# Rebuilding the order of the first tile in a fused attention and feed-forward kernel

## The chip, the cores and the metric

The kernel runs on one core of one Trainium2 chip, as one launch. The metric is the device time of that launch in microseconds; lower is better. Five runs of the kernel before stand beside one profiled execution.

## The reference, cut to what matters

Block-causal attention over 8 batches of 8 heads, 576 positions and 64 elements a head (blocks of 64 positions), then a gated feed-forward layer on the same 4608 tokens. All inputs and the output are float32.

```python
scores = scale * np.matmul(q, k.transpose(0, 1, 3, 2))      # scale = 1/8
mask = (pos[:, None] // 64) >= (pos[None, :] // 64)
attn = softmax(np.where(mask, scores, -1e9))
x = np.matmul(attn, v).transpose(0, 2, 1, 3).reshape(4608, 512)
gate = np.maximum(x @ w_gate, 0.0)                          # w_gate, w_val: 512 x 1536
out = (gate * (x @ w_val)) @ w_out                          # w_out: 1536 x 512
```

## The kernel before

**Attention.** A *round* `r` is a pair of heads of one batch: batch `r // 4`, pair `hp = r % 4`. For 512 of the 576 positions it needs q and k with the head's elements on the partitions (`qTm`, `kTm`), computes scores transposed, takes exp on ACT into `attnT`, sets the corners that the mask forbids to zero (`corners`), multiplies with v (`head_av`, one head each; a column of ones beside v gives the sum), normalises on DVE (`normalise`: a reciprocal and a multiply into `xnat`), and transposes the result into `xT`, the input of the feed-forward layer. The last 64 positions of all batches are *tails*: `tail_visit`, `tail_av`, `xTt`.

**Feed-forward.** `ffn_gen` is a Python generator over nine tiles `j`: one for each batch's 512 positions and one for all tails. Each `next` puts one 128x512 matmul into PE's program, so a tile has 144 steps: for `f` in 0 to 11 four products for gate and four for val (one for each chunk `c` of `xT`, that is for each round of the batch), then four out-projections of twelve. ACT takes the relu of gate, DVE multiplies it with val into `hT`, DVE copies the out-projection to `ob`, which a DMA stores. Attention work of batch `j + 1` and later stands between these steps at positions that are written out by hand: `ffn(n)` goes on by `n` steps, and `run(base, events)` sorts pairs of position and function.

**The order is by hand on every engine**: `tc.manual_schedule` keeps the order in which the program emits instructions on PE, DVE, ACT, POOL and SP. An engine that waits holds all that is behind it. Semaphores between engines are set by the framework, which also orders two engines' accesses to one PSUM bank.

**PSUM** has eight banks: `sc` two tiles of two banks, `one` one bank, and `ffnp` three banks, which gate, val, out-projection, transposes, `head_av` and a part of each score visit share.

**Loads.** All early loads are issued on SP's queue in the order of need (batch 0, weights, batch 1, w_out, batch 2), land as float32 in ten `stage` buffers, and are cast to bf16 by an engine: `cast_qk`, `cast_v`, `cast_w`, mostly on POOL. A stage buffer is loaded again when its cast is done. From batch 3 or 4 on, loads are issued by POOL and cast by the DMA (`load_qkv`), and transposes are DMAs on SP (`dma_transposes`, `to_xT_dma`).

**Batch 0 and the first tile.** Rounds 0 to 3 are done before the feed-forward layer starts, in a loop over `r`: `scores_1`, `pe_mains` of the next round (transposes on PE, L281, copied by `evac` at L284), `scores_2`, `head_av` of an earlier round. `junk` puts matmuls on zeros into PE's program. The first step of tile 0 is position 0. Batch 1's `pe_mains` stand at positions 64, 68, 98 and 110, its `sort_v` (v loaded packed, put in order by matmuls with a selection matrix) at 72 and 116, rounds 4 to 7 at 76, 88, 100 and 118. The stores of tile 0 are issued by POOL, all others by ACT.

Lines that the following text names: L182 `cast_qk`, L195 `cast_v`, L281 and L284 `pe_mains`, L316 `load_qkv`, L363 `cast_w`, L426 scores of `visit`, L508 the multiply of `normalise`, L553 `head_av`, L573 to L578 `to_xT_pe`, L583 `to_xT_dma`, L615 gate and val products, L624 relu, L628 `hT`, L634 out-projection, L664 `junk`.

Of the kernel before, what the change touches and what calls it, by code (L numbers as in the profile page):

```python
# [17 lines left out]
def kernel(  # L18
# [10 lines left out]
    nc = tc.nc  # L29
# [36 lines left out]
    attnT = [consts.tile([128, 2, AW], BF, name=f"attnT{i}") for i in range(2)]  # L66
# [52 lines left out]
    class Early:  # L119
# [59 lines left out]
        def cast_qk(self, h0, n, engs):  # L179
            lo = 64 * (h0 % 4)  # L180
            for t in range(2):
                engs[t](  # L182
                    self.half(t, h0 // 4)[:, :, lo : lo + 64 * n].rearrange(
                        "p j (h d) -> p h j d", d=64
                    ),
                    self.st[t, h0].rearrange("p (h j d) -> p h j d", h=n, j=4),
                )
# [60 lines left out]
        def transpose(self, hg):  # L248

            for t in range(2):  # L250
                pm = sb.tile([128, 4, 2, 128], BF, name="perm", bufs=8)
# [23 lines left out]
        def pe_mains(self, hp, evac):  # L275
            for t in range(2):
# [3 lines left out]
                for j in range(4):  # L280
# [3 lines left out]
                evac[t](  # L284
                    (qTm, kTm)[t][self.b % 2][:, :, hp, :].rearrange(
                        "p c (n j) -> p c n j", j=4
                    ),
                    tp.rearrange("p (j c n) -> p c n j", j=4, c=4),
                )
# [96 lines left out]
    def scores_1(r):  # L386
        b, hp = divmod(r, 4)
        at = attnT[r % 2]
        sc = scores(b, hp, [(0, 0, True)])
        nc.scalar.activation(at[:, :, 0:512], sc, AF.Exp, scale=scale)  # L390
        sc = scores(b, hp, [(0, 1, True), (384, 3, True)])
        return lambda: nc.scalar.activation(
            at[:, :, 512:1024], sc, AF.Exp, scale=scale
        )

    def scores_2(r):
        at = attnT[r % 2]
        sc = scores(*divmod(r, 4), [(0, 2, True)])
        nc.scalar.activation(
            at[:, :, 1024:1280], sc[:, :, 0:256], AF.Exp, scale=scale  # L400
        )
# [10 lines left out]
    def visit(r):  # L412

        b, hp = divmod(r, 4)
        at = attnT[r % 2]
# [74 lines left out]
    def corners(r, eng):  # L490

        at = attnT[r % 2]
        for lo, n in ((0, 512), (896, 128)):
            two = at[64:128, :, lo : lo + 2 * n].rearrange("p g (c n) -> p g c n", c=2)
            eng.memset(two[:, :, :, 0:64], 0.0)

    def corner(r, c, eng):
        eng.memset(attnT[r % 2][64:128, :, BASE[c] : BASE[c] + 64], 0.0)
# [39 lines left out]
    def head_av(r, hh):  # L538
        b, hp = divmod(r, 4)
        h = 2 * hp + hh  # L540
        at = attnT[r % 2]
# [20 lines left out]

    def xT_of(b):
# [4 lines left out]
    def to_xT_pe(r, evac):  # L568
        b, hp = divmod(r, 4)
        br = psum_ffn.tile([128, 1024], BF, name="ffnp")  # L570
# [3 lines left out]
        if r == 3:  # L574
# [27 lines left out]
    def ffn_gen():  # L602
        for j in range(B + 1):
            hT = []
            x = xT_of(j) if j < B else xTt.rearrange("p b h n -> p h b n")
            for f in range(12):
                i, fo = f // 4, 128 * (f % 4)
                gate = psum_ffn.tile([128, 512], FP, name="ffnp")
                val = psum_ffn.tile([128, 512], FP, name="ffnp")
                steps = [(t, c) for t in range(2) for c in range(4)]  # L610
                if j == 0 and f == 0:

                    steps.sort(key=lambda tc_: tc_[1] == 3)
                for t, c in steps:
                    nc.tensor.matmul(  # L615
                        (gate, val)[t],
                        (wg, wv)[t][i][:, c, fo : fo + 128],
# [3 lines left out]
                    )  # L621
                    if (t, c) == (0, 3):
# [4 lines left out]
                h = sb.tile([128, 512], BF, name="hT", bufs=16)  # L627
# [40 lines left out]
    dve, act, pool = nc.vector.tensor_copy, nc.scalar.copy, nc.gpsimd.tensor_copy  # L668
    with tc.manual_schedule(engines={E.PE, E.DVE, E.Activation, E.Pool, E.SP}):
# [11 lines left out]
        e0.cast_qk(0, 2, (dve, act))  # L681
        e0.pe_mains(0, (dve, act))
        junk(2)
        constants(1, nc.gpsimd)
        for h0 in (2, 4, 6):
            e0.cast_qk(h0, 2, (pool, pool))
        for r in range(4):
            scores_1(r)()
            if r == 3:
                e0.cast_v(6, 2, pool)  # L690
# [246 lines left out]
```

## Time and profile before

| | us |
|---|---|
| median of five runs | 372.78 |
| lowest and highest | 372.62, 378.24 |
| the profiled execution, its own time | 372.62 |
| span of that execution in the trace | 370.8 |
| first feed-forward matmul (L615) | 20.36 |
| first step of tile 1 (L615) | 66.56 |
| busy in the span: PE, ACT, DVE, POOL | 357.5, 171.2, 170.1, 119.1 |

The page shows one execution on this core. A row of an engine in the 40 slices gives the busy share of each slice of 9.27 us in tenths. A row of a list of stretches begins with the stretch and its length, and has for PE, PEld, DVE, ACT and POOL busy time and count, then the granted clock, the DMA share and GB/s. A wait row names who waited for whom: total, times, longest. A timeline row has start, duration, engine, line, operation, tiles and shape, and in brackets the idle time before it and what ended that.

### The profile page before, as it was taken

To read this page: it belongs to the slowest core of one execution; us is meant where nothing else is said; L and a number is where in the kernel's file an instruction comes from. 1 tells how busy PE (TensorE), PEld (TensorE's weight loads), DVE (VectorE), ACT (ScalarE), POOL (GpSimd) and SP (SyncE) were. 2 spreads that over 40 slices of the span, in tenths; PEclk is the share of its full clock that TensorE was granted. 3 is DMA by queue.
4 is the path that set the end of the run, shared out by engine and by line. 5 is a ranking of instruction groups with operands and counts; after the bars stand their busy time and mean duration, and the time that the engine had idled before them with its cause. 6 is when DMAs were issued, how large, how long until landed. Compare 5 with 4: busy or idle time off the path is not lost.

```text
span 370.8 us, 7561 instructions
## 1 busy us (share of the span) xinstructions
PE 357.5 (96%) x3004; PEld 177.3 (48%) x3004; DVE 170.1 (46%) x392; ACT 171.2 (46%) x283; POOL 119.1 (32%) x156
## 2 busy tenths in 40 slices
PE   6799979999999999999999999999999999999995
PEld 2544445544555545444554455444544454444443
DVE  3634444447465544444445533555254443423422
ACT  5933745566536462466345544553465323302310
POOL 6688866356258084580076004000000000000000
PEclk9999999999999999999999999999999999999999
DMA  8999999969959899999799857545200220020013
GB/s 254 292 371 356 375 205 296 211 173 253 163 135 132 87 132 172 149 126 154 150 102 129 139 120 84 44 90 124 80 14 17 67 77 6 2 85 28 3 38 104
DMA packets 140739, 51.35 MB, mean 138 GB/s; under 512 B 120352, under 2 KB 133920, under 8 KB 140704
## 3 DMA queue, kind: packets, MB, share of 16 engines
q0 software_dynamic: 56576, 8.13, 43.8%
q1 hardware_dynamic: 79424, 34.62, 42.7%
q10 hardware_dynamic: 4704, 8.13, 6.8%
q8 instruction: 23, 0.38, 0.4%
q14 instruction: 12, 0.10, 0.1%
HBM read 37.75 MB, written 9.44 MB: 127 GB/s over the span
## 4 chain that ended last, share of the span: by engine, by line
PE 83%; DMA 10%; POOL 2%; issue 1%; DVE 1%; ACT 1%; SPq 1%; POOLq 0%; ACTq 0%
PE ffnp L615 45%; PE ffnp L634 24%; PE ffnp L553 5%; DMA stage<-in_moe_w_val_dram 3%; DMA stage<-in_k_dram 3%; PE sc L426 3%; PE ffnp L522 2%; DMA xT<-xnat 2%; PE one L426 1%; DMA stage<-in_q_dram 1%; PE sc L460 1%; POOL k_bf L182 1%; SPq L132 1%; POOL sel L94 1%; POOL q_bf L182 0%
## 5 line engine op out<-in xcount | busy, mean ns | idle before, releaser
L628 DVE TENSOR_TENSOR hT<-gate_sb,ffnp 128x512 bf16<-128x512 bf16 x108 | 74.1, 686 | 95.8 <-PE ffnp L615 80.4
L624 ACT ACTIVATE gate_sb<-ffnp 128x512 bf16<-128x512 f32 x108 | 65.1, 603 | 101.5 <-PE ffnp L615 101.5
L615 PE MATMUL ffnp<-xT,wg 128*128 128x512 bf16 x384 | 102.1, 380 | 0.8 <-DMA xT<-xnat 0.8
L615 PE MATMUL ffnp<-xT,wv 128*128 128x512 bf16 x384 | 102.1, 380 | 0.3 <-ACT gate_sb L624 0.2
L634 PE MATMUL ffnp<-wo,hT 128*128 128x512 bf16 (+1 forms) x444 | 102.4, 374 | 0.0
L615 PEld LDWEIGHTS <-wv 128*128 128x128 bf16 x432 | 40.1, 98 | 47.1 <-issue 3.8
L615 PEld LDWEIGHTS <-wg 128*128 128x128 bf16 x432 | 40.0, 98 | 46.5 <-issue 3.2
L634 PEld LDWEIGHTS <-hT 128*128 128x128 bf16 x444 | 40.2, 98 | 40.0 <-issue 0.8
L435 ACT ACTIVATE attnT<-sc 128x1024 bf16<-128x1024 f32 x56 | 57.0, 1042 | 0.0
L644 DVE COPY ob<-ffnp 128x512 f32<-128x512 f32 (+1 forms) x37 | 25.0, 677 | 40.7 <-PE ffnp L634 40.6
L316 POOL DMA_DIRECT2D v_bf<-in_v_dram x20 | 16.8, 858 | 61.3 <-PE ffnp L522 47.7
L553 PEld LDWEIGHTS <-attnT 128*128 128x128 bf16 x640 | 26.4, 98 | 15.7 <-DVE xnat L508 4.4
L507 DVE RECIPROCAL recip<-ffnp 128x4 f32<-128x4 f32 (+1 forms) x76 | 13.6, 179 | 37.1 <-PE ffnp L553 26.7
L553 PE MATMUL ffnp<-v_bf,attnT 128*128 128x65 bf16 x600 | 28.2, 194 | 0.1
L441 ACT ACTIVATE attnT<-one 128x256 bf16<-128x256 f32 x28 | 10.7, 382 | 35.2 <-PE ffnp L426 21.4
L508 DVE TENSOR_TENSOR xnat<-ffnp,recip 128x256 bf16<-128x256 f32 x60 | 25.5, 424 | 2.1
L426 PE MATMUL sc<-qTm,kTm 64*128 64x512 bf16 (+1 forms) x168 | 16.9, 305 | 0.0
L426 PEld LDWEIGHTS <-kTm 64*128 64x128 bf16 x224 | 8.9, 94 | 14.9 <-issue 10.6
L481 ACT ACTIVATE attnTt<-one 64x256 bf16<-64x256 f32 x8 | 3.0, 376 | 28.0 <-PE ffnp L460 28.0
L472 ACT ACTIVATE attnTt<-sc 128x1024 bf16<-128x1024 f32 x16 | 15.6, 1016 | 0.0
L316 POOL DMA_DIRECT2D k_bf<-in_k_dram x16 | 14.2, 907 | 3.1 <-DMA v_bf<-in_v_dram 2.8
L316 POOL DMA_DIRECT2D q_bf<-in_q_dram x16 | 14.3, 920 | 2.0 <-DMA k_bf<-in_k_dram 1.8
(88 smaller groups left out, 260.9 us busy)
## 6 DMA issues: line engine op xcount, KB each, us to landing
out_dram<-ob ACTq DMA_DIRECT2D x28, 256.0 KB, 2.3
stage<-in_moe_w_gate_dram SPq DMA_DIRECT2D x6, 512.0 KB, 9.3
stage<-in_moe_w_val_dram SPq DMA_DIRECT2D x6, 512.0 KB, 9.5
stage<-in_q_dram SPq DMA_DIRECT2D x6, 512.0 KB, 6.6
stage<-in_k_dram SPq DMA_DIRECT2D x6, 512.0 KB, 7.7
stage<-in_moe_w_out_dram SPq DMA_DIRECT2D x6, 512.0 KB, 9.0
stage<-in_v_dram SPq DMA_DIRECT2D x8, 256.0 KB, 6.9
q_bf<-in_q_dram POOLq DMA_DIRECT2D x16, 128.0 KB, 6.4
```

Source lines behind the costliest of these rows:

```text
L316: nc.gpsimd.dma_start(dst, src[b, :, 128 * c : 128 * c + n, :].rearrange("h p d -> p h d"),)
L426: nc.tensor.matmul(where[c].rearrange("p (c n) -> p c n", n=128), kTm[b % 2][head_of(hh), c, hp, :], qTm[b % 2][head_of(hh), c:4, hp, :], ...
L435: return lambda: nc.scalar.activation(at[:, :, lo : lo + 512], sc, AF.Exp, scale=scale)
L472: return lambda: nc.scalar.activation(at[:, :, 2 * i : 2 * i + 2, 0:256], main[i].rearrange("p g (h n) -> p g h n", h=2), AF.Exp, scale=scale,
L507: nc.vector.reciprocal(recip, av[:, :, 64])
L508: nc.vector.tensor_tensor(out=out, in0=av[:, :, 0:64], in1=recip.to_broadcast([rows, n, 64]), op=AX.mult,)
L553: nc.tensor.matmul(av[:, p, :], at[:, hh, col : col + 128], vb[:, c, h, :], start=(p == 0), stop=(c == p), skip_group_check=True,)
L615: nc.tensor.matmul((gate, val)[t], (wg, wv)[t][i][:, c, fo : fo + 128], x[:, c], start=(c == 0), stop=(c == 3),)
L624: nc.scalar.activation(gate_sb, gate, AF.Relu)
L628: nc.vector.tensor_tensor(out=h, in0=gate_sb, in1=val, op=AX.mult)
L634: nc.tensor.matmul(op, hT[f][:, 128 * s : 128 * (s + 1)], wo[f // 4][:, f % 4, n0:n1], start=(f == 0), stop=(f == 11),)
L644: nc.vector.tensor_copy(ob, op)
```

## The change

The change rewrites the hand-made order of the first tile and what follows from it:

- `scores_1` and `scores_2` become `part(r, i)`, one exp each, and the loop over `r` becomes a list. q of round 0 is cast by ACT and k by DVE; the copy of its k out of PSUM is split between ACT and DVE. POOL's casts of v and of the last k piece are put between the zeroings of corners; the corners of round 3 are zeroed by ACT.
- `junk(2)`, `junk(5)` and `junk(2)` behind the first ones are taken out.
- In tiles 0 and 1 the generator emits, at `f = 0`, nine products on chunks 0 to 2 (gate, val and the gate of `f = 1`, which is held in a third buffer `ahead`) in front of the first product on chunk 3.
- Between those nine products and chunk 3 stands the last round of the batch, with both heads in one PSUM tile and one normalisation (`both_av`), for rounds 3 and 7. Their transposes use the `one` bank.
- Batch 1: `pe_mains` at 78, 82, 122, 124, rounds at 94, 109, 127, 138, `sort_v` at 90; k cast by DVE at 72 and 119; the second half of v is loaded in its final order (`load_v`), so its `sort_v` is gone.
- Batch 2's q and k are loaded ahead of tails; its casts and DMA transposes are in two parts (`mains_2a`, `mains_2b`); most casts of tails and of tail v come after POOL's stores of tile 0.
- Later tiles: the tail of batch 0 moves from 4 to 10 and `pe_tails` of batch 1 from 7 to 100 (tile 1); the tail of batch 2 from 50 to 3, two rounds and the v load of batch 4 move (tile 3).
- Buffers: `attnT` 4 instead of 2, `perm` 4 instead of 8, `hT` 13 instead of 16.

The diff, cut to its core:

```diff
-    attnT = [... for i in range(2)]
+    attnT = [... for i in range(4)]
-    def scores_1(r): ...
-    def scores_2(r): ...
+    def part(r, i):
+
+        pieces = [[(0, 0, True)], [(0, 1, True), (384, 3, True)], [(0, 2, True)]][i]
+        sc = scores(*divmod(r, 4), pieces)
+        w = (512, 512, 256)[i]
+        nc.scalar.activation(
+            attnT[r % 4][:, :, 512 * i : 512 * i + w], sc[:, :, 0:w], AF.Exp, scale=scale
+        )
...
+    def both_av(r):
+
+        b, hp = divmod(r, 4)
+        xnats[r] = sb.tile([128, 4, 128], BF, name="xnat", bufs=3)
+        both = psum_sc.tile([128, 2, 512], FP, name="sc")[:, :, 0:260]
+        av = both.rearrange("q g (p e) -> q g p e", e=65)
+        for hh in range(2):
+            for p in range(4):
+                for c in range(p + 1):
+                    col = BASE[c] + 128 * (p - c)
+                    nc.tensor.matmul(
+                        av[:, hh, p, :],
+                        attnT[r % 4][:, hh, col : col + 128],
+                        v_bf[b % 2][:, c, 2 * hp + hh, :],
+                        start=(p == 0),
+                        stop=(c == p),
+                        skip_group_check=True,
+                    )
+        recip = sb.tile([128, 2, 4], FP, name="recip_both", bufs=1)
+        nc.vector.reciprocal(recip, av[:, :, :, 64])
+        nc.vector.tensor_tensor(
+            out=xnats[r].rearrange("q p (g d) -> q g p d", g=2),
+            in0=av[:, :, :, 0:64],
+            in1=recip.to_broadcast([128, 2, 4, 64]),
+            op=AX.mult,
+        )
...
-        br = psum_ffn.tile([128, 1024], BF, name="ffnp")
+        if hp == 3:
+            br = psum_one.tile([128, 1024], BF, name="one")
+        else:
+            br = psum_ffn.tile([128, 1024], BF, name="ffnp")
...
+                steps = [(t, c) for t in range(2) for c in range(4)]
+                if ahead is None:
+                    gate = psum_ffn.tile([128, 512], FP, name="ffnp")
+                else:
+                    gate, ahead, steps = ahead, None, steps[3:]
+                val = psum_ffn.tile([128, 512], FP, name="ffnp")
+                if j < 2 and f == 0:
+                    ahead = psum_ffn.tile([128, 512], FP, name="ffnp")
+                    for c in range(3):
+                        product(gate, 0, c, 0)
+                        yield
+                    for c in range(3):
+                        product(val, 1, c, 0)
+                        yield
+                    for c in range(3):
+                        product(ahead, 0, c, 1)
+                        yield
+                    steps = [(0, 3), (1, 3)]
...
-        e0.cast_qk(0, 2, (dve, act))
-        e0.pe_mains(0, (dve, act))
-        junk(2)
+        e0.cast_qk(0, 2, (act, dve))
+        e0.pe_mains(0, (dve, [(act, 0, 1), (dve, 1, 4)]))
...
+        part(2, 0)
+        e0.pe_mains(3, (dve, dve))
+        part(2, 1)
+        e0.cast_v(2, 2, pool)
+        head_av(0, 0)
+        head_av(0, 1)
+        part(2, 2)
+        part(3, 0)
+        e0.cast_v(4, 2, pool)
+        corners(2, zero_pool)
+        head_av(1, 0)
+        head_av(1, 1)
+        part(3, 1)
+        to_xT_pe(0, (dve,))
+        part(3, 2)
+        corners(3, zero_act)
+        e0.cast_v(6, 2, pool)
         cast_w(w_0[0], pool)
-        head_av(3, 0)
-        head_av(3, 1)
-        junk(5)
-        to_xT_pe(3, (act, dve))
-        junk(2)
+        head_av(2, 0)
+        head_av(2, 1)
+        to_xT_pe(1, (dve,))
+        to_xT_pe(2, (act,))
+        ffn(9)
+        both_av(3)
+        to_xT_pe(3, (act, dve))
...
-        for r, p in ((4, 76), (5, 88), (6, 100), (7, 118)):
-            end = 20 if r == 6 else 14
-            events += round_at(p, r, (p + end + 2, p + end + 6), (p + end + 10, pe_xT))
+        events = round_at(94, 4, (113, 117), (121, pe_xT))
+        events += round_at(109, 5, (129, 133), (137, pe_xT))
+        events += round_at(127, 6, (142, 143), (144, pe_xT))
+        events += round_at(138, 7, (153, None), (153, pe_xT))
         events += [
-            (98, lambda: e1.pe_mains(2, (dve, act))),
-            (110, lambda: e1.pe_mains(3, (dve, act))),
-            (111, load_2),
-            (116, lambda: e1.sort_v(4, (dve, act))),
-            (124, mains_2),
-            (140, lambda: e0.pe_tails((dve, act))),
+            (72, lambda: e1.cast_qk(0, 4, (None, dve))),
+            (78, lambda: e1.pe_mains(0, (dve, act))),
+            (82, lambda: e1.pe_mains(1, (dve, act))),
+            (90, lambda: e1.sort_v(0, (dve, act))),
+            (119, lambda: e1.cast_qk(4, 4, (None, dve))),
+            (122, lambda: e1.pe_mains(2, (dve, act))),
+            (124, lambda: e1.pe_mains(3, (dve, act))),
+            (133, mains_2a),
+            (143.5, lambda: e0.pe_tails((dve, act))),
         ]
         run(0, events)
-        events = tail_at(4, 0, (20, 24)) + tail_at(116, 1, (132, 136))
+        events = tail_at(10, 0, (26, 30)) + tail_at(116, 1, (132, 136))
...
-            (8, tails_2),
+            (9.5, mains_2b),
+            (22, tails_2),
...
-                events += tail_at(50, 2, (69, 73))
-            for i, p in enumerate((2, 26, 74, 96) if b == 3 else (2, 32, 62, 92)):
+                events += tail_at(3, 2, (21, 25))
+            for i, p in enumerate((27, 50, 73, 96) if b == 3 else (2, 32, 62, 92)):
```

`mains_2a` casts the first half of batch 2's q and k on POOL, issues two DMA transposes, and loads the v tail of batch 0 and a half of batch 2's v. `mains_2b` does the same for the second half, then loads all tails of batches 2 and 1, and casts the v tail of batch 0. `tails_2` casts and transposes the tails of batch 2 and casts those of batch 1 with their v.

## The prediction

> **What bounds the kernel now.** I read the page first, then busy time by stretch, then PE's waits, then the timeline at the places that the waits name.
>
> ```profile
> PE 357.5 (96%) x3004; PEld 177.3 (48%) x3004; DVE 170.1 (46%) x392; ACT 171.2 (46%) x283; POOL 119.1 (32%) x156
> PE   6799979999999999999999999999999999999995
> GB/s 254 292 371 356 375 205 296 211 173 253 163 135 132 87 132 172 149 126 154 150 102 129 139 120 84 44 90 124 80 14 17 67 77 6 2 85 28 3 38 104
> ```
>
> PE is the engine. Only the first two slices, the sixth and the last are not full. Up to 46 us (slices three to five, 356 to 375 GB/s) the loads run near their highest rate.
>
> ```profile
> 20.00:33.00 13.00, 13.00 (x63) 5.90 (x61) 4.70 (x8) 4.55 (x8) 10.24 (x13) 1.00 1.08 362
> 33.00:51.00 18.00, 14.55 (x127) 7.01 (x126) 8.25 (x18) 10.05 (x18) 13.90 (x15) 1.00 1.10 331
> 51.00:67.00 16.00, 15.75 (x167) 8.19 (x164) 8.07 (x23) 8.61 (x15) 10.23 (x14) 1.00 1.02 274
> ```
>
> The second number is PE's busy time. 20 to 33 is full; 33 to 51 lacks 3.45 us. The waits name the cause:
>
> ```profile
> PE ffnp L281 <- POOL k_bf L182: 1.9, 2, 1.3
> PE ffnp L281 <- POOL q_bf L182: 0.9, 2, 0.7
> PE ffnp L615 <- DMA xT<-xnat: 0.8, 1, 0.8
> PE one L553 <- POOL v_bf L195: 0.8, 1, 0.8
> ```
>
> L281 is a transpose of batch 1, placed in the middle of FFN tile 0 before its input has landed:
>
> ```profile
> 46.69 0.59 PE L634 MATMUL ffnp<-wo,hT 128*128 128x512 bf16 x2
> 48.03 0.40 PE L281 MATMUL ffnp<-ident,q_bf 128*128 128x128 bf16 x4 [0.74 <-POOL q_bf L182]
> 49.75 0.40 PE L281 MATMUL ffnp<-ident,k_bf 128*128 128x128 bf16 x4 [1.32 <-POOL k_bf L182]
> 49.98 0.60 PE L634 MATMUL ffnp<-wo,hT 128*128 128x512 bf16 x2
> ```
>
> A busy PE hides small holes, since a 128x512 matmul lasts 380 ns but starts every 216 (in the chain of waits 96 of L615 take 20.72 us). So I take start to start, less 216 ns for 512 columns. By that count 0.4 (at 34.0), 0.75 (34.7), 0.4 (37.0), 0.5 (38.1), 0.9 (46.9), 1.5 (48.2) and 0.5 (54.0 to 55.0) are lost: 4.9 us in tile 0. In all it loses more: from 20.36 to 66.56 there are 144 steps (31.2) and 9.0 of inserted PE work (four transposes of batch 1 at 0.445, two sorts at 0.55, four score visits at 0.65, eight head_av at 0.30, four xT at 0.22, tails 0.25), so 6.0 of 46.2 is lost, 1.1 of it in holes too small to list. One more stands late, 1.0 us at 149.97, where tile 3 waits for its last attention chunk, which took 7.9 us to be transposed by DMA:
>
> ```profile
> 149.97 0.39 PE L615 MATMUL ffnp<-xT,wg 128*128 128x512 bf16 x1
> 151.17 0.38 PE L615 MATMUL ffnp<-xT,wg 128*128 128x512 bf16 x1 [0.81 <-DMA xT<-xnat]
> ```
>
> **The sum's base.** The profiled execution took 372.62 us with a span of 370.8, so 1.8 lies around the span. It is 0.16 under the median of 372.78. I add to and take from 372.62.
>
> **The change, part by part.** A "position" p is a step of the FFN generator, 216 ns.
>
> *Start (before the FFN).* What the new order does to ACT: the twelve exps cost 1.02, 1.02, 0.60 us but start 0.91, 0.90, 0.59 apart, 2.4 us a round; before, ACT waits 0.90 and 0.49 us for scores. q is now cast on ACT (0.62 against DVE's 0.43) and k on DVE; the copy of k is split, so the first exp starts near 6.6 against 6.79. Round 1 is then held by DVE's copies of its q and k (2 x 0.69, ending 8.62 as now), so it starts near 9.15 against 9.20. From there it is dense: rounds 2 and 3 at 11.7 and 14.1 (12.53 and 15.30 now), the last exp ending near 16.6 against 17.8. So far a gain of 1.2 us. But DVE now has, in this order: copies of round 3 to 13.3; two heads of round 0 (0.60 each) to 14.5; round 1 to 15.7; xT(0), 0.42 by my estimate (a 256 column copy is 0.29, half the columns of 0.13 more); round 2 from 16.15 to 17.35; xT(1) to 17.8; ACT copies xT(2) (0.60) to 18.45. The nine products put ahead (3 for gate, 3 for val, 3 for the next gate) need these: the third starts near 18.5, the ninth ends near 20.0. Their weights are there: the val half landed at 17.06 and its POOL cast takes 1.04. Only then comes both_av(3). From its start to the first product on chunk 3: 20 matmuls, 0.76 to the last one's end; reciprocal 0.19; the 512 element multiply 0.69 (the row of hT, the same size; 256 elements take 0.42); then as now from xnat to a copied xT, 1.25 (19.63 to 20.82, and a release). With releases, 2.95 us, of which PE works 0.82. So chunk 3 starts near 22.95 with 9 steps done. Before, 9 steps were done at 22.30. The start is 0.65 us later in effect, though the exps end earlier, because two-headed normalisation is behind nine products and nothing is left for PE. And since gate, val and ahead hold all three ffnp buffers, the next val waits for the first relu (0.60): 0.4 more. Sum: 1.05 us lost. Nine of the sixteen junk matmuls go; they stood in such holes, and their going moves nothing by itself.
>
> *Clock.* Row: the first seven junk matmuls take 3.17 us, 0.43 apart; from 5.5 us on they are 0.22 apart, and stay so after the 1.5 us hole at 48.2 and in the thin stretch 10 to 16 us. [...]
>
> *Batch 1 in tile 0.* Transposes, rounds and sort go from positions 64, 68, 72, 76 to 78, 82, 90, 94, and the later ones to 122, 124 and 109, 127, 138. By my clock position 78 falls at 38 us (its k cast is due about 36, landed 32.8), 122 at 51.5; the last k piece lands at 48.6, its cast now being DVE's (0.85, twice the 0.43 row; DVE has 0.69 of work per 1.73 us of FFN, so it fits, but were the landing late, the hT multiplies behind it would stop, and PE after three buffers). So these holes go. What comes: two PSUM buffers are asked for while gate and val hold two of three, 0.3 us at 78 to 82 and 0.3 at 122 to 124 (before, 0.4 at 37.0 and 0.5 at 54 for the same); 0.5 at 142 to 144, where two head_av, the tail transposes and xT(6) meet within two steps. Together 1.1. A floor stands under this: the last w_out half is cast at 45.43 to 46.47, behind its DMA, and position 106 needs it; I have 106 at 46.75, so a faster start would bring little. Of the 1.1 of small holes I keep half, 0.5.
>
> *sort_v(4) goes*: 16 matmuls, 0.55. In its place v is loaded in 256 byte rows on SP: four transfers for one. At the start such 128 KB pieces land 0.60 apart, so 2.4 us for the half against 2.1 for the packed one. It is needed only at position 142; nothing waits.
>
> *Round 7 at position 153.* Before, tile 1 started with all its chunks. Now nine products run, then both_av(7): the same 2.95 us with 0.82 of work, a hole of 2.13. At position 154 the tail scores need an ffnp buffer, which is released only by the first relu: 0.8 more. Sum 2.9 lost. I find no work that covers it: PE's order has nothing else there.
>
> *Queues.* SP: batch 2's q and k now go ahead of the tails; its four transposes are cut in two pairs, at 133 and 153; six tail loads are behind the second pair. POOL: the three cast_v_tail and half of the tail casts go behind; the stores of tile 0 stand ahead of these and are issued near 55 instead of 56.28, so ob's third buffer comes free in time. I take 0: transposed q and k of batch 2 land about 62 for a use at 68 (before, POOL waited 2.2 for them at 72.2).
>
> *Tiles 1 to 3.* The tail of batch 2 goes from 50 to 3, so the v load of batch 4, which waits on POOL for tail_av (47.7 us in its waits), starts near 118 instead of 129.3, and the q and k loads behind it move up as well. By 143 those packets should be through, and the last xT transpose takes nearer its median of 2.9 us than 7.9, with 6.7 to spare: 1.0 gained. A 0.3 wait at 121.93 near that tail: half gained.
>
> *At nothing*: four attnT and four perm buffers, thirteen hT (PE is in order, and hT of the tile before was read 12 matmuls earlier), corners on ACT (2 x 0.3 after its last exp).
>
> Sum: to the end of position 153, 6.0 of losses and 0.55 of sort go; 1.05 (start), 1.1, 0.5 and 2.9 come: 1.0 gained. With 1.0 and 0.15 in tiles 1 to 3: 2.15. 372.62 - 2.15 = 370.5 (370.6 on the median).
>
> **Rivals.** *Holes covered* (0.2): the stalls go and the two both_av holes are short, as if xT came without the wait. For it: the nine products ahead stand where xT is waited for. Against: nothing follows both_av in PE's order, and in tile 0 the floor at position 106 allows 0.3. 370.5 - 2.1 - 0.8 - 0.3 = 367.3. *The holes eat it all* (0.15): stalls are swapped for holes and tile 3 still waits: 370.5 + 1.0 + 1.0 = 372.5. *POOL behind the tails* (0.13, slower): un(2,1)'s k half is on POOL behind batch 1's tail casts, whose loads are last on SP after two transposes and four v pieces. Issued at 0.6 us apiece they land about 74; but v pieces took 2.87 and 3.14 us each at 55.80 and 58.76 with a full queue. If they land at 82, un(2,1) ends at 83.9, and round 9's scores, due at 78.7, wait 5.2: 375.7. It decides from a landing of about 77, and turns the result slower from 79.7. That the change doesn't do what it says: the late placing is plain in the order, so this is part of the second rival.
>
> **How the numbers follow.** Likeliest 0.52 at 370.5. What a measurement of this kernel can tell from no change is 0.2%, 0.75 us. Faster 0.74: the likeliest with nearly all its own range, the first rival, a little of the second. Same 0.11: most of the second. Slower 0.15: the last rival, and the clock on top of the second. Range 367.5 (nearly all of the holes covered) to 373.5 (all eaten, half of the clock's price).
>
> **What would show it.** Exps without a hole of ACT from 9 to 16.6; first three products near 17.7 to 18.7; PE idle about 2.1 us before both chunk 3 products, with DVE's 512 element multiply and ACT's xT copy in the hole; no L281 waits for POOL; last xT of tile 3 landing before 149. It is wrong if those two holes are under a microsecond, if PE waits for POOL's kTm after 75, or if matmuls stand 0.43 apart after 20.

## The result and the profile after

The kernel after takes 376.97 us (median of 25 runs, 374.55 to 380.02); the kernel before, run beside it, 373.43 (46 runs). The ratio is 1.009, 95% interval 1.007 to 1.011: slower by 3.5 us, where the forecast was 370.5. Medians here are of all runs; ratios leave out the few runs that were over 1.5% above the fastest of their kernel. The profiled execution of after took 377.13 us, its span is 375.0.

The first lines to read are those of the page that stood in the prediction for before, and one more, the granted clock:

```profile
PE 359.6 (96%) x2979; PEld 177.7 (47%) x2979; DVE 172.3 (46%) x392; ACT 170.4 (45%) x282; POOL 116.0 (31%) x151
PE   6879899799999999999999999999999999999995
PEclk9889999899999999999999999999999999999999
```

PE has 25 instructions less and is busy 2.1 us longer. Its thin slices behind the start are now the third, fifth and eighth, and in the second, third and eighth slice the clock is not full. In before that last row is

```profile
PEclk9999999999999999999999999999999999999999
```

The list of stretches shows how much; the last but two number of a row is the granted clock:

```profile
10.00:15.00 5.00, 4.29 (x47) 2.56 (x47) 3.35 (x8) 3.99 (x7) 3.08 (x7) 0.66 1.26 261
20.00:33.00 13.00, 10.94 (x63) 4.96 (x61) 4.19 (x8) 3.25 (x6) 9.32 (x12) 0.87 1.08 362
25.00:30.00 5.00, 5.00 (x17) 1.96 (x16) 1.79 (x3) 0.78 (x2) 3.43 (x5) 0.66 1.10 349
33.00:51.00 18.00, 17.06 (x108) 7.76 (x106) 8.95 (x15) 8.24 (x14) 12.15 (x13) 1.00 1.02 319
70.00:80.00 10.00, 8.32 (x91) 4.28 (x92) 3.75 (x8) 5.06 (x9) 5.15 (x7) 0.83 1.06 139
```

A clock of 0.66 over 5 us, or 0.83 over 10, is 3.4 us at half rate. There are three such stretches: from 11.36 to 14.78, 25.02 to 28.43 and 72.80 to 76.22. From 25 to 30 PE is busy the whole time and starts only 17 matmuls. From 33 to 51, where before lost most, the stalls are nearly gone: 17.06 busy of 18 against 14.55.

PE's waits, in after:

```profile
PE one L597 <- DVE xnat L577: 2.1, 2, 1.0
PE ffnp L634 <- DVE xT L600: 1.6, 2, 0.8
PE ffnp L283 <- DVE k_bf L184: 0.7, 1, 0.7
PE ffnp L457 <- ACT gate_sb L664: 0.6, 1, 0.6
PE ffnp L283 <- ACT xT L602: 0.5, 1, 0.5
```

The waits for POOL's casts and for tile 3's DMA transpose that the prediction showed are gone. The first two lines in their place are the two `both_av` holes (L597 are its transposes, L634 the gate and val products), the fourth is the tail score that waits for a PSUM buffer (the third comes in experiment 6; the fifth waits for a PSUM buffer too). In the timeline the first hole and what follows it read so:

```profile
20.70 0.77 PE L567 MATMUL sc<-v_bf,attnT 128*128 128x65 bf16 x20
21.52 0.21 DVE L576 RECIPROCAL recip_both<-sc 128x8 f32<-128x8 f32 x1 [3.12 <-PE sc L567]
21.76 0.69 DVE L577 TENSOR_TENSOR xnat<-sc,recip_both 128x512 bf16<-128x512 f32 x1
22.50 0.40 PE L597 MATMUL one<-ident,xnat 128*128 128x128 bf16 x4 [1.03 <-DVE xnat L577]
22.94 0.37 ACT L599 COPY xT<-one 128x256 bf16<-128x256 bf16 x1 [3.79 <-PE one L597]
23.34 0.29 DVE L600 COPY xT<-one 128x256 bf16<-128x256 bf16 x1 [0.90 <-ACT xT L599]
23.69 0.38 PE L634 MATMUL ffnp<-xT,wg 128*128 128x512 bf16 x1 [0.79 <-DVE xT L600]
23.90 0.38 PE L634 MATMUL ffnp<-xT,wv 128*128 128x512 bf16 x1
24.12 0.38 PE L634 MATMUL ffnp<-xT,wg 128*128 128x512 bf16 x1
24.75 1.22 PE L634 MATMUL ffnp<-xT,wv 128*128 128x512 bf16 x3 [0.25 <-ACT gate_sb L664]
```

Start to start, less each matmul's own time, 1.19 us are lost before the transposes and 0.95 behind them, and 0.41 at 24.12, where val waits for the first relu. The last row shows what the prediction named as the sign of a slow clock: from 24.96 on eight products follow 0.427 apart instead of 0.216, though none waits for anything. The same chain repeats in tile 1: 1.19 and 0.95 from 69.12 to 71.53, 0.74 for the tail's PSUM buffer, and products 0.427 apart from 73.59 to 76.12.

### The profile page after: what moved, and what is told of

Its sections match the earlier page's. It is cut to its first block, busy times and chain, and to the rows that moved or that the text cites. A ratio compares the mean times of both kernels' runs of the same rounds, so it can differ in the third digit from the quotient of the medians.

```text
span 375.0 us, 7492 instructions
## 1 busy us (share of the span) xinstructions
PE 359.6 (96%) x2979; PEld 177.7 (47%) x2979; DVE 172.3 (46%) x392; ACT 170.4 (45%) x282; POOL 116.0 (31%) x151
## 4 chain that ended last, share of the span: by engine, by line
PE 93%; DVE 3%; ACT 1%; DMA 1%; issue 0%; DVEq 0%
PE ffnp L634 51%; PE ffnp L674 25%; PE ffnp L547 5%; PE sc L423 3%; PE ffnp L516 3%; PE one L423 2%; PE ffnp L283 1%; PE sc L457 1%; DMA stage<-in_q_dram 1%; PE sc L380 1%; DVE qTm L289 1%; DVE kTm L289 0%; PE one L457 0%; PE one L547 0%; DVE k_bf L184 0%
## 5 line engine op out<-in xcount | busy, mean ns | idle before, releaser
L634 PE MATMUL ffnp<-xT,wg 128*128 128x512 bf16 x384 | 104.8, 383 | 2.1 <-DVE xT L600 1.6
L634 PE MATMUL ffnp<-xT,wv 128*128 128x512 bf16 x384 | 104.6, 386 | 0.3 <-ACT gate_sb L664 0.3
L634 PEld LDWEIGHTS <-wv 128*128 128x128 bf16 x432 | 40.5, 99 | 48.8 <-issue 6.9
L634 PEld LDWEIGHTS <-wg 128*128 128x128 bf16 x432 | 40.5, 98 | 47.1 <-issue 5.0
L547 PEld LDWEIGHTS <-attnT 128*128 128x128 bf16 x600 | 25.0, 99 | 14.5 <-DVE xnat L502 4.4
L547 PE MATMUL ffnp<-v_bf,attnT 128*128 128x65 bf16 x570 | 27.0, 195 | 0.0
L502 DVE TENSOR_TENSOR xnat<-ffnp,recip 128x256 bf16<-128x256 f32 x57 | 24.2, 424 | 2.0
L423 PE MATMUL sc<-qTm,kTm 64*128 64x512 bf16 (+1 forms) x168 | 17.0, 305 | 0.0
L423 PEld LDWEIGHTS <-kTm 64*128 64x128 bf16 x224 | 9.0, 94 | 15.3 <-issue 11.7
```

The costliest lines, as they stand in the source:

```text
L423: nc.tensor.matmul(where[c].rearrange("p (c n) -> p c n", n=128), kTm[b % 2][head_of(hh), c, hp, :], qTm[b % 2][head_of(hh), c:4, hp, :], ...
L502: nc.vector.tensor_tensor(out=out, in0=av[:, :, 0:64], in1=recip.to_broadcast([rows, n, 64]), op=AX.mult,)
L547: nc.tensor.matmul(av[:, p, :], at[:, hh, col : col + 128], vb[:, c, h, :], start=(p == 0), stop=(c == p), skip_group_check=True,)
L634: nc.tensor.matmul(to, (wg, wv)[t][f // 4][:, c, 128 * (f % 4) : 128 * (f % 4) + 128], x[:, c], start=(c == 0), stop=(c == 3),)
```

## The experiments

The theory from these lines: **the holes set the clock back, and that is most of the loss**. Rivals: the holes themselves are (the clock only shows them), the nine junk matmuls that were taken out are (they would have kept the clock), or work behind the holes is. Ratios are to the kernel before on the same chip.

**1. Fill the holes with matmuls on zeros, and change nothing else.** Nobody waits less; only the clock can gain.

```diff
+    def junk_sc(n): ...        # n 128x512 matmuls on zeros into a tile of sc
         both_av(3)
+        junk_sc(5)
         to_xT_pe(3, (act, dve))
+        junk_sc(4)
...
-        events += round_at(138, 7, (153, None), (153, pe_xT))
+        events += round_at(138, 7, (153, None), (153, lambda r: (junk_sc(5), pe_xT(r), junk_sc(4))))
```

> The changed kernel, with nine matmuls on zeros put back into each of the two holes that both_av leaves (five before the transposes, four behind them), in an sc tile. The order of all other work is unchanged and the holes stay as long as they are (1.19 + 0.95 us each). Theory clock: the holes cost twice, once by themselves and once because the granted clock falls to a half for 3.4 us behind each; with PE kept active the two half-rate windows near 25 and 73 us vanish (mean clock 0.986 to 0.995) and the time falls by 1.6 + 1.4 = 3.0 us, to about 374. Rival order: the loss is the holes and the waits alone and the clock is a side show that the next wait absorbs; no change, 377 +- 0.7.

Measured: 374.63 (22 runs), ratio 1.0019 (0.9998 to 1.0040), 2.3 us under after. In its profile no stretch is at half rate; the stretches:

```profile
25.00:30.00 5.00, 4.95 (x24) 2.24 (x23) 1.99 (x3) 1.79 (x3) 3.43 (x5) 1.00 1.10 349
70.00:80.00 10.00, 9.79 (x120) 5.29 (x122) 5.00 (x11) 7.01 (x12) 3.66 (x6) 1.00 1.04 139
```

24 matmuls start from 25 to 30 in place of 17. The timeline shows that the hole is as it was, with L704, the junk, in it:

```profile
20.57 1.03 PE L704 MATMUL sc<-v_p,ident 128*128 128x512 bf16 x4
20.80 0.69 DVE L577 TENSOR_TENSOR xnat<-sc,recip_both 128x512 bf16<-128x512 f32 x1
21.55 0.40 PE L597 MATMUL one<-ident,xnat 128*128 128x128 bf16 x4
22.73 0.38 PE L634 MATMUL ffnp<-xT,wg 128*128 128x512 bf16 x1
```

So the clock's part is shown apart from the holes: 2.3 us by the medians. With DVE's multiplies into `hT` as marks, in us later than before:

```
mark                     before    after    holes filled (warm)
tile 0, f = 0             22.70    +2.03    +1.07
tile 0, f = 3             27.54    +3.48    +0.84
tile 0, f = 11            46.65    +1.76    -0.89
tile 1, f = 3             76.19    +5.00    +0.73
tile 1, f = 5             80.40    +4.95    +2.49
tile 8, last ob copy     367.08    +4.19    +1.45
```

(In tile 0 work was moved across the marks, so only rows of one mark compare.) After loses to `warm` 0.96 up to the first mark, 1.69 in the second half-rate stretch and 1.61 in the third, 4.26 in all. The first 0.96 lies ahead of all the junk that `warm` adds: that its start kept the clock is chance, not the junk's work, so the two filled holes stand for 3.30 in these two profiles. But between `f = 3` and `f = 5` of tile 1 `warm` gives 1.8 back. Where that goes is seen in the third experiment.

**2. End the first hole earlier.** The first six products ahead go behind `both_av(3)`, so that DVE normalises while PE multiplies.

```diff
-        ffn(9)
         both_av(3)
+        ffn(6)
         to_xT_pe(3, (act, dve))
+        ffn(3)
```

> The changed kernel, with one thing moved in front of tile 0: both_av of round 3 is emitted ahead of the nine products, its transposes behind six of them, three products last. Theory holes: the nine products now cover the normalisation; chunk 3 starts near 21.5 us instead of 23.7 and no half-rate window follows: 2.2 + 1.6 = 3.8 us less, about 373, the hole in tile 1 remaining. Rival floor: what is gained at the start is given back at the next input that lands late (batch 1 casts, w_out), so at most 1.5 us less, 375.5.

Measured: 375.76 (21 runs), ratio 1.0064 (1.0038 to 1.0089): 1.2 us under after by the medians, though the intervals of the two ratios overlap. The profile shows the mark `f = 0` of tile 0 at 21.55, 1.16 ahead of before, and no half rate in tile 0. The stretch after tile 1's hole is still at half rate (69.91 to 73.32), and between `f = 3` and `f = 5` of tile 1 another 1.7 us are lost. Against after it is 3.7 ahead at the first `ob` copy, 3.3 at `f = 3` of tile 1, and 1.6 at `f = 5`: the gain is made and half of it is given back, as the rival had it.

**3. End both holes earlier.** As 2, and round 7's `both_av` at 147 with its transposes at 151.

```diff
-        events += round_at(138, 7, (153, None), (153, pe_xT))
+        events += round_at(138, 7, (147, None), (151, pe_xT), 2, 4)     # third exp and corners 2 and 4 steps behind
```

> As the kernel that moves round 3 ahead of its nine products, and the same for round 7: its second exp at position 140 instead of 144, corners at 142, both_av at 147, transposes at 151. Theory holes: the hole at position 153 shrinks from 2.1 to about 0.6 and the half-rate window behind it goes: 1.4 + 1.4 = 2.8 us below the kernel with round 3 alone, about 370.5, and faster than the kernel before. Rival: round 7's exps are not done by 147, so PE waits there as long as it did at 153; no more than 0.5 us below the kernel with round 3 alone.

Measured: 375.58 (22 runs), ratio 1.0041 (1.0015 to 1.0067). In its profile PE runs at half rate early (9.35 to 16.18) and nowhere later; tile 1's hole has shrunk to 0.33 and 0.52, and at `f = 3` of tile 1 it is 0.14 ahead of before. Then this:

```profile
78.99 0.61 POOL L219 CAST v_bf<-stage 64x512 bf16<-64x512 f32 x1 [1.51 <-DMA stage<-in_v_dram]
79.09 2.52 DVE L268 COPY qTm<-perm 128x512 bf16<-128x512 bf16 x1
79.55 1.06 POOL L268 COPY kTm<-perm 128x512 bf16<-128x512 bf16 x1
80.56 0.61 POOL L219 CAST v_bf<-stage 64x512 bf16<-64x512 f32 x1
81.67 0.27 PE L423 MATMUL one<-qTm,kTm 64*128 64x256 bf16 x1 [0.70 <-DVE qTm L268]
```

POOL waits 1.51 us for a tail's v. `un(2,1)` puts q and k of one round of batch 2 in order by two copies; its k half is behind that cast in POOL's order, its q half on DVE takes 2.52 us beside POOL instead of 0.60 alone, and round 9's scores (L423) wait; with what follows, 1.8 us are lost. This is the prediction's slow rival, "POOL behind the tails", in small. In after it can't be seen, since PE comes there 5 us later. In tile 3 the wait for the last DMA transpose is back, too (0.94 at 150.76).

**4. Take the nine junk matmuls out of before.**

```diff
-        junk(2)
...
-        junk(5)
...
-        junk(2)
```

> The kernel before, with the nine junk matmuls behind the first seven taken out and nothing else. Theory clock by activity: PE's stretch from 16 to 20 us then holds little but short matmuls and transposes, and in a part of the executions the clock falls to a half for 3.4 us once or twice: 0.5 to 1.7 us slower in the mean, 374 to 375. [...]

Measured: 373.23 (22 runs), ratio 0.9982 (0.9959 to 1.0005). Its profile has one stretch at half rate (11.71 to 15.12), and that costs no time that can be measured. So the missing junk is by itself not what makes after slow: the profile is 0.79 behind before at `f = 0` of tile 0 and 0.15 at `f = 11`, as the time goes into the waits for landings at 35 to 50 us that before has anyway.

**5. After, with before's start.** `scores_1` and `scores_2`, the loop over `r`, two `head_av` for round 3 and the junk are put back; tiles 0 and 1 are as in after.

```diff
-        part(0, 0)
-        part(0, 1)
...
-        ffn(9)
-        both_av(3)
+        for r in range(4): ...          # as in before, L664 with it
```

> The start of the kernel before (its loop over the four rounds, head_av of round 3 and the junk matmuls in front of the first product), with everything of the changed kernel from the weight casts on: late batch 1, both_av of round 7 at position 153, the new queues. Theory start: the new start costs 3.5 us by the end of its half-rate window (2.4 + 1.1), and it alone makes the change slower than the kernel before; without it the stalls are gone and the time falls to about 374 (less the 1.8 us that come back at batch 2's k, as seen in the kernels with a mended start). Rival tile 1: the loss is made in tile 1 as well, so that an old start still leaves it 1 us above the kernel before: 375.

Measured: 374.63 (12 runs), ratio 1.0039 (1.0009 to 1.0069). Its profile has half rate from 12.50 and from 70.53. The rest of the change alone is 1.4 us slower than before: tile 1's hole (1.19, 0.95), its PSUM wait (0.74) and its slow stretch are in it unchanged.

**6. k's casts back on POOL.** In after, the wait for k that the prediction meant to have removed is still there, as the third line of the waits says:

```profile
40.26 1.50 DVE L184 CAST k_bf<-stage 128x1024 bf16<-128x1024 f32 x1
41.52 1.12 POOL L368 CAST wo<-stage 128x1024 bf16<-128x1024 f32 x1 [0.32 <-DMA stage<-in_moe_w_out_dram]
41.81 0.40 PE L283 MATMUL ffnp<-ident,k_bf 128*128 128x128 bf16 x4 [0.75 <-DVE k_bf L184]
43.49 0.38 PE L283 MATMUL ffnp<-ident,k_bf 128*128 128x128 bf16 x4 [0.19 <-DVE hT L668]
```

DVE's cast takes 1.50 us beside POOL's casts of w_out; the same cast at 54.80, with POOL idle, took 0.68. PE loses 0.91 in this wait. The next transposes of k lose 0.36 more, but the cast was done 1.7 us earlier: DVE's multiply into `hT`, which frees a PSUM buffer, ended that wait.

```diff
-        e1.cast_qk(0, 4, (pool, None))
+        e1.cast_qk(0, 4, (pool, pool))
...
-            (72, lambda: e1.cast_qk(0, 4, (None, dve))),
...
-            (119, lambda: e1.cast_qk(4, 4, (None, dve))),
```

> The changed kernel with batch 1's two casts of k back on POOL and nothing else. Theory DVE: the cast at position 72 took 1.50 us on DVE beside POOL's casts (0.68 at position 119 beside an idle POOL), and PE waited 0.91 and 0.36 us for it; on POOL it is done long before, so 1.0 to 1.3 us less, 375.8. Rival POOL: POOL gets 2 us more work while the w_out casts fall due, position 106 waits for them, no gain.

Measured: 377.07 (6 runs), ratio 1.0114 (1.0094 to 1.0135). Its trace shows the two waits (0.91 and 0.36 in after) at 0.19 and 0.26, yet no time came of it: the profile has half rate from 7.88 to 18.12 and is 2.15 behind after at the first mark. Six runs can't tell 1 us apart from the changing start (below), so its worth by itself stays open.

**7. The give-back taken out.** As 3, with batch 1's tail loads behind `un(2,1)` and their casts later.

```diff
-            e1.cast_tails((pool, pool))
-            e1.cast_v_tail(pool)
...
-            (44, un(2, 1, (dve, pool))),
+            (40, un(2, 1, (dve, pool))),
+            (41, lambda: (e1.load_tails((0, 1)), e1.load_tails((2,)))),
+            (54, lambda: (e1.cast_tails((pool, pool)), e1.cast_v_tail(pool))),
```

> The kernel with both rounds moved ahead of their products, and batch 1's tails taken out of the way of batch 2: their loads at 144 + 41 and their casts at 144 + 54, un(2,1) at 144 + 40. Theory give-back: in the kernel with both rounds moved, PE waited 0.86 + 0.58 + 0.41 us near 82 us since POOL's part of un(2,1) stood behind a tail that landed at 78.9 and DVE's part took 2.5 us beside POOL; without it 1.8 us less than that kernel, about 373.8. Rival: the next input (round 10's, or a clock window) takes the same time; no change.

Measured: 374.12 (8 runs), ratio 1.0044 (1.0020 to 1.0068). The median is 1.5 us under that of 3, which ran on another chip, but the ratio is no lower than its 1.0041, so whether time came of it stays open. The wait at 79 to 82 is gone from its trace; one of 0.80 and 0.57 at 92.9 to 94.4 is new. Its profile fell on a late start: PE comes to full rate only at 17.74.

**8. All mends together.** As 7, k on POOL, and the second half of tile 0 spread.

```diff
-        events += round_at(109, 5, (129, 133), (137, pe_xT))
-        events += round_at(127, 6, (142, 143), (144, pe_xT))
-        events += round_at(138, 7, (147, None), (151, pe_xT), 2, 4)
+        events += round_at(105, 5, (126, 129), (133, pe_xT))
+        events += round_at(123, 6, (138, 141), (145, pe_xT), 4)
+        events += round_at(133, 7, (146, None), (150, pe_xT), 2, 5)
...
-            (122, lambda: e1.pe_mains(2, (dve, act))),
-            (124, lambda: e1.pe_mains(3, (dve, act))),
+            (110, lambda: e1.pe_mains(2, (dve, act))),
+            (120, lambda: e1.pe_mains(3, (dve, act))),
```

> All of the mends together: round 3 and round 7 ahead of their products, k casts on POOL, tails of batch 1 late, and the second half of tile 0 spread so that no two steps ask for the same ffnp buffer (round 5 at 105, transposes at 110 and 120, round 6 at 123, tails at 131, round 7 at 133, both_av at 146). Theory sum: 377.0 less 3.0 (clock), 2.2 (start hole), 1.4 (tile 1 hole), 1.0 (k cast), 1.0 (buffers): 368.5 to 370. Rival landing: round 5 and the transposes at 105 to 110 come before k has landed (48.6 us), and the earlier start is given back there: 371.5 to 373.

Measured: 373.53 (22 runs), ratio 1.0005 (0.9983 to 1.0026). All that after had lost is back, and nothing more. Its profile has again the late start (17.84), 0.84 lost at 53.42, 0.59 at 91.7 and 1.2 for tile 3's DMA at 149.41.

**9. Is the start a lottery?** The first seven junk matmuls last 3.17 us, less than a stretch of 3.41, and in the profiles with them PE comes to full rate at 4.5 to 5.9 us or (7 and 8) only at 17.8. Two variants of before: without the seven, and with eight that start earlier and six more in rounds 0 and 1.

```diff
-        junk(7)                                # before_cold
...
-        junk(7)                                # before_warm
+        junk(8, left=zeros[:, 0:128])
...
+            junk_one(1)
```

> The kernel before without its first seven junk matmuls. Theory (the start's clock is a lottery: seven matmuls last 3.17 us, less than one window of 3.41 us, so whether they turn PE to full rate depends on where the windows fall): PE comes to full rate later, at 8 to 12 us or at the dense exps' scores, in most executions; about 1.5 to 2 us slower, near 375.2, and in the profile the matmuls before 8 us stand 0.43 apart. Rival (the start is bound by loads and by ACT's exps, whatever PE's rate, and the spread of the times is something else): within 0.5 us of 373.6.

> The kernel before with eight junk matmuls in place of seven, which start some 0.45 us earlier (zeros as weights, so they don't wait for the identity), and six more in PE's gaps of rounds 0 and 1. Theory (start lottery): PE is at full rate by 8 us in every execution, the mean is 0.7 us lower and the runs lie closer together. Rival (the added matmuls delay the scores that ACT waits for, and the spread has another cause): no gain, 373.6 to 374.2, and the same spread.

Measured: 373.35 (14 runs), ratio 1.0000 (0.9968 to 1.0033), and 373.25 (14 runs), 0.9998 (0.9966 to 1.0029), with the same spread as before (standard deviations 1.5, 1.4 and 1.4). The first profile has PE at half rate up to 14.28, and `f = 0` of tile 0 is 1.17 later; by the first `ob` copy 0.43 of that are left. So the start is a lottery in the trace, but in before it decides nothing, and the theory that the runs' spread comes from it falls. That profile fell on a long wait for tile 3's last chunk, and shows by chance what followed a hole of more than 3 us:

```profile
150.41 0.39 PE L615 MATMUL ffnp<-xT,wg 128*128 128x512 bf16 x1
153.79 0.38 PE L615 MATMUL ffnp<-xT,wg 128*128 128x512 bf16 x1 [2.99 <-DMA xT<-xnat]
```

```profile
155.00:160.00 5.00, 5.00 (x27) 2.19 (x26) 1.68 (x4) 1.97 (x3) 3.20 (x4) 0.74 3.30 127
```

3.17 us are lost in the wait, where before lost 0.98 at the same place; behind it PE is at half rate from 154.21 on, which costs 1.7 more. The landing of this one transpose alone put this execution 3.9 us back.

**10. A version to beat both.** As 8, with junk in the start (for a full clock), tile 3's last chunk four steps earlier, and batch 1's last transposes at 110 and 114.

```diff
-        junk(7)
+        junk(8, left=zeros[:, 0:128])
+        junk_one(2)
...
-        events = round_at(94, 4, (113, 117), (124, pe_xT))
+        events = round_at(94, 4, (118, 121), (125, pe_xT))
...
-            (120, lambda: e1.pe_mains(3, (dve, act))),
+            (114, lambda: e1.pe_mains(3, (dve, act))),
...
-            for i, p in enumerate((27, 50, 73, 96) if b == 3 else (2, 32, 62, 92)):
+            for i, p in enumerate((24, 46, 69, 92) if b == 3 else (2, 32, 62, 92)):
```

> The kernel after with its two both_av holes ended earlier (the chunk is normalised ahead of the gate's products), k's casts on POOL, batch 1's tails behind un(2,1), the second half of tile 0 spread (transposes at 114, head_av at 118 and 121, tails at 136), tile 3's last chunk four steps earlier, and junk matmuls in the start. Theory: with the clock at full rate from the start and the give-backs gone (start 1.7, 0.8 at 53, 1.2 at 149 of the run before it), 371 to 372, below both kernels. Rival (each gain runs into a landing): 373.5, as the kernel before.

Measured: 372.64 (22 runs), ratio 0.9992 (0.9970 to 1.0014). At `f = 3` of tile 1 its profile is 1.3 us ahead of before. Then 2.2 go between `f = 9` and `f = 10`:

```profile
89.88 2.94 DVE L268 COPY qTm<-perm 128x512 bf16<-128x512 bf16 x1
90.33 1.06 POOL L268 COPY kTm<-perm 128x512 bf16<-128x512 bf16 x1
91.35 1.03 POOL L184 CAST q_bf<-stage 128x1024 bf16<-128x1024 f32 x1
```

Again a DVE copy (`un(2,3)`) beside POOL's casts, and round 11's scores behind it.

**11. That wait taken out as well**, and the transposes at 115 and 122.

```diff
-            (80, un(2, 3, (dve, pool))),
+            (68, un(2, 3, (dve, pool))),
```

> The run before it (best2) with three moves: un(2,3), which stood among POOL's casts (its DVE copy took 2.94 us and PE waited 1.28 and 0.57), twelve steps earlier; batch 1's last two transposes at 115 and 122, where their k has landed (PE waited 1.9 at 48.4 to 49.9); head_av(4) at 112 and 118. Theory (these two stalls are what is left of the gains): 1.5 to 2 us below best2, near 371, ratio to the kernel before about 0.995. Rival (the loads set the time that tile 0 and tile 1 can end, and the next landing takes what is gained): 372.6, as best2.

Measured: 373.61 (22 runs, 370.48 to 378.20), ratio 0.9991 (0.9967 to 1.0014). The rival was right. PE's waits in its profile:

```profile
PE ffnp L634 <- DMA xT<-xnat: 3.4, 3, 1.6
PE ffnp L283 <- POOL k_bf L184: 1.4, 2, 0.9
PE one L423 <- POOL kTm L268: 1.1, 1, 1.1
```

At `f = 3` of tile 1 it is 1.8 ahead of before. Then 1.3 go to `un(2,2)`, now the late one, at 86.2, 1.3 to a DMA transpose of tile 2 at 110.2, and 0.9 and 1.8 to tile 3's DMA transposes at 151 to 153. No version that was run beats before by what the runs can tell; the last three of after (8, 10, 11) stand level with it.

## Why the prediction was wrong

**The clock (the failed step).** The forecast's sum has no term for the clock. "Half of the clock's price" in its range and "the clock on top of the second" in its chances stand on 1.7 us for one stretch at half rate, which no run of before shows; in after such a stretch behind a hole cost 1.69 and 1.61. Three stretches came, for 4.3 us in the profiled execution (0.96 of it in the start), and filling the two holes brought 2.3 back in the median (experiment 1), of the 6.4 by which the median missed the forecast's 370.6; the other 4 are in the terms below. Not every execution had three: over the 25 runs of after the granted clock is 0.982 to 0.995, never full (in `warm` 0.989 to 1.000), and one stretch alone makes it 0.995. Thirteen runs have no more than that, yet they take 374.6 to 378.4, so what spreads the runs stays open.

The row that the prediction rested on was read too kindly. The 1.5 us hole at 48.2 in before stands behind one of 0.9 at 46.9, in one stretch that kept the clock by a hair, as the table shows. What sorts the traces is PE's work over a whole stretch of 3.41 us, the length of each of the three half-rate stretches of after (3.413 in the clock records of its trace). These start 13.66 and 47.78 us apart, 4 and 14 times that length, so a window here is a stretch of that grid. The windows ahead of half rate were not idle. Adding up PE's work in each window of the grid (each matmul's own time at full rate, 0.056 us for 128 columns and 0.216 for 512, or the time to the next start if that is less) gives:

```
kernel          window from   PE's work   without transposes   next window
after                  7.95        0.38                 0.23   half
after                 21.61        0.33                 0.27   half
after                 69.39        0.20                 0.14   half
start                 66.50        0.31                 0.24   half
before_nojunk          8.30        0.31                 0.18   half
oldstart               9.09        0.34                 0.21   half
before_cold          150.79        0.12                 0.12   half
both                   5.94        0.39                 0.26   half
kpool                  4.47        0.35                 0.13   half
start                  5.06        0.38                 0.16   full
before                45.99        0.39                 0.33   full
before_nojunk          4.89        0.39                 0.16   full
warm                   4.99        0.39                 0.16   full
before_nojunk         45.85        0.41                 0.35   full
best2                 47.14        0.43                 0.30   full
warm                   8.40        0.48                 0.23   full
```

These are windows at full rate with low shares. Under 0.38 a window at half rate followed, over 0.39 none did; at 0.38 and 0.39 either is seen. The same sum sorts the windows that are themselves at half rate: 0.35 (`both`) and 0.37 and 0.35 (`kpool`) were followed by another, 0.44 to 0.58 by full rate. PE was busy there for 0.65 to 0.69 and for 0.84 to 1.00 of the window, since matmuls of 512 columns follow 0.427 apart there instead of 0.216; so it is either the columns that count, or PE must be busier to gain the clock than to keep it, and no run separates the two.

Two holes of 1.19 and 0.95 us, each far under 3.4, with 0.2 of transposes between them and the PSUM wait behind them, bring a window to 0.33 or 0.20. The prediction had these holes to the tenth of a microsecond, one behind the other, and gave them no price in the clock. The third column sorts worse than the second (0.27 lost the clock, 0.16 and 0.23 kept it), so the transposes seem to count in this kernel. That is read from the windows and was not tried by itself.

**The start** was sized 1.05 later to the first mark of tile 0; chunk 3 came at 23.69 instead of 22.95. With the clock full (`warm`) it came at 22.73 and the first mark 1.07 later, so this 0.74 is clock too. In `warm` the exps are as dense as forecast (the last ends at 16.5 for 16.6); in after the half-rate stretch opens two holes of 0.5 between them, and the last ends at 17.4. The chain from `both_av` to chunk 3 took 2.99 us for 2.95, and val's wait 0.41 for 0.4.

**k's cast on DVE** was put at 0.85 us from an uncontended row and cost 1.50 beside POOL; PE lost 0.91 where nothing was foreseen. The prediction counted DVE's work, not what POOL does beside it.

**PSUM buffers** were sized 1.1 and took 2.3: 0.36 at 78 to 82 for 0.3, 1.03 at 122 to 124 for 0.3, and 0.87 at 142 to 144 for 0.5.

**Right:** the old stalls went; tile 1's hole lost 2.14 (2.13 foreseen) and its tail scores 0.74 (0.8); and behind the first matmuls POOL held PE nowhere in after.

**Right by luck:** tile 3 no longer waits for its DMA (0.98 gone, 1.0 foreseen), but the reason given did not come true. The last transpose, meant to take near 2.9 us and to land before 149, was issued at 148.75 and landed at 155.72, after 7.0; in `warm`, where PE is 2.7 earlier, it landed at 151.01, against 151.13 in before. PE came to that chunk in after at 155.7, late enough to find it. Where PE came earlier with the same order, the wait was back (0.94 in `both`, 1.2 in `best1`).

**The sum.** Up to `f = 3` of tile 1 the forecast was 1.0 earlier than before, the trace is 5.0 later. Of these 6.0, 4.26 are clock (start included), 0.91 is k's cast and 1.16 the PSUM buffers beyond their 1.1, less 0.2 for the start at full clock: 6.1. From there on, 1.15 was to be gained and 0.8 was.

**And without the clock?** `warm` has all the rest of the change and is still no faster than before (1.0019); its profile ends 1.45 later, not the 2.15 earlier of the forecast. Of these 3.6, 0.9 is k's cast, 1.2 the buffers, and 1.8 is what the prediction called its slow rival: as soon as PE is early enough, it meets the tail's landing. In 8, 10 and 11 other landings and casts take what each further mend gains. The floor that the prediction put under position 106 alone (a landing, not PE, sets the time) stands at several places up to 153 us. How much of it is the landings themselves, and how much DVE and POOL holding each other up, no run separates.

## What to carry to other kernels

Ask of the clock not how long each hole is, but how much PE does in the worst 3.41 us: here every window under 0.38 lost it and none over 0.39 did. Two short holes (1.19 and 0.95 us) with transposes between them made one cold window, and its price (1.6 to 1.7 us) came on top of the holes. Where a hole can't be filled with work, matmuls on zeros in it were worth their place here (2.3 us in the median), and they are the experiment that separates the clock from the wait. When stages are bound by landings, a gain in one stage is only worth what the next landing leaves of it: look for the first load or cast that the earlier PE will reach, before adding gains up.

## What the hardware did that was not expected

- Half rate followed windows in which PE had work for 0.12 to 0.39 of the time, as above. And in three profiles PE was at half rate early (up to 14.28 us in `before_cold`, 17.74 in `both_un`, 17.84 in `best1`) without a sign of it in the granted clock: in `both_un` it reads 1.00 from 5 to 10 us, while 128x128 transposes stand 0.107 apart instead of 0.056.
- A VectorE copy within SBUF of 128x512 bf16 took 0.60 us alone and 2.52 and 2.94 beside POOL's copies and casts; a cast of 128x1024 0.68 and 1.50. Of 112 such copies (128x512) in the 14 traces 41 last over 0.7 us, and 40 of these end 0.44 to 0.47 after a POOL cast or copy ended. Where DVE came first it took 0.60, and POOL's copy took 1.49 and 1.35 instead of 1.06 (before, 72.16 and 118.04). Why the one holds the other up, no run shows.
- Tile 3's last DMA transpose took 7.9 us and held PE for 0.98 in before; in `before_cold`, the same program but for the first junk, it took 10.0 and held PE for 3.17.
